# DeltaNet attention with a feed-forward block: other matmuls inside the bursts of 32x32 products, and state products with 48 weight columns

## The chip, the cores and the metric

The kernel runs on one core of a Trainium2 chip. The metric is the device time of that core in microseconds, for the whole launch. The tensor engine (TensorE, PE in the profile) multiplies and writes into PSUM; VectorE (DVE) and ScalarE (ACT) compute on SBUF and PSUM; GpSimd (POOL) has little to do here, and SyncE (SP) issues nearly all DMAs. A weight load of the tensor engine is listed separately as PEld.

## The reference

The first half is a delta rule with a running state per batch and head; its output, regrouped to tokens by features, goes through a feed-forward block with a learned slope for negative values.

```python
# q, k, v: (4, 8, 768, 48), beta: (4, 8, 768)
k_n = k / (norm(k) + 1e-6)
state = zeros((B, H, D, D))
for t in range(S):
    y[:, :, t] = einsum('bhd,bhde->bhe', q[:, :, t], state)
    v_old = einsum('bhde,bhd->bhe', state, k_n[:, :, t])
    state += beta_t * einsum('bhd,bhe->bhde', k_n[:, :, t], v[:, :, t] - v_old)
x = y.transpose(0, 2, 1, 3).reshape(3072, 384)
h = x @ w_in                                  # w_in: (384, 2048)
g = maximum(h, 0) + alpha * minimum(h, 0)
out = g @ w_out                               # w_out: (2048, 384)
```

Everything is float32.

## The kernel before

**Chunks and steps.** The sequence of 768 is cut into 12 chunks of 64 positions. A step `n` is one chunk of two of the four batches, so there are 24 steps, and the step's 16 problems (two batches, eight heads) are packed by halves of 64 partitions: `half(t)` is a half, `dims(a)` the first 48 partitions of one. Within a chunk the recurrence is a triangular system. Its matrix comes from products of keys with keys (`grams`), its inverse is built from blocks of 32, and then each step does: `through_state` (keys and queries times the state), `solve` (inverse times right side, giving `u`), `outputs`, and `next_state`, which adds keys times `u` to the state. `to_ffn` transposes the step's output into `xt`, the left operand of the feed-forward block.

**The 32x32 inverses.** Four steps form a group, whose 32x32 diagonal blocks VectorE inverts together by elimination. For the first group `eliminate_small` does only blocks of 16, and `cross` joins two inverted blocks of 16 into one of 32 by products of 32x32 weights with 16 columns, one per block and partition quarter: a burst at line 540, a copy by ScalarE (`half_way`), then two bursts at lines 549 and 555, and additions by VectorE (lines 561 and 563). `first_chunk` runs one `cross` over the blocks of the first two steps; two later ones, each over eight blocks, do steps 2 and 3. `between_1` and `between_2` (lines 621 and 636) then build the inverse of 64 from those of 32, with operands that ScalarE places by line 586.

**Fillers.** `busy(n)` (line 974) issues matmuls of the identity with 512 columns per unit of `n` into a PSUM tile that nobody reads. `first_chunk` calls it between its stages.

**Feed-forward.** `ffn_in(c)` multiplies `xt` of chunk `c` by `w_in` (line 809, 128x128 weights and 256 columns, 48 parts per chunk), twelve matmul records to a PSUM bank; ScalarE (line 819) and VectorE (line 821) then apply the activation and free the bank. Two banks alternate. `ffn_out` and `ffn_out_fast` (lines 851 and 873) multiply by `w_out`.

**Weights.** `w_in` and `w_out` come in pieces, fetched by SP (line 191) as space becomes free, and rewritten by ScalarE (lines 207, 208) and VectorE (lines 217, 222).

**Order.** Each engine runs its instructions in the order in which the program issues them: the schedule is written out by hand. `first_chunk` is straight code. After it, `weave` merges several generators: each has a number of parts, and the one whose share of parts done is smallest goes next, so that all of them advance evenly. The weave at line 1182 merges `ffn_in(0)`, the two later `cross` (taken alternately by `in_turn`, two parts each) followed by `ready(2)` and `pair(2)` (steps 2 and 3), the weight conversions, and the keys of the next group (`statics`). From step 4 on a loop weaves one step of attention with feed-forward parts and a share of the next group's elimination. All attention products use PSUM tiles `p_big`, of which there are three in rotation.

**A product in the trace.** Each float32 product appears as two weight loads and two matmul records, so 16 products of a step are 32 records. Only the transposes count once.

**The state.** `state[bp]` holds, for two batches, 48 rows in the first part of each half of 64 partitions; the keys of `k_late` are padded with zeros from 48 to 64 columns, so the product at line 707 fills 64 partitions of each half, and the rows beyond 48 are zero.

## Time and profile before

| | us |
|---|---|
| Median of 6 runs | 692.17 |
| Lowest and highest | 690.47 and 694.42 |
| The profiled execution's own time | 693.02 |
| Its span in the profile | 691.2 |
| Busy: TensorE, weight loads | 671.0, 581.9 |
| Busy: VectorE, ScalarE, GpSimd | 450.3, 248.7, 19.3 |
| Mean granted clock of TensorE | 0.985 |

The profile is one execution. Its page gives busy time by engine, a row of digits for 40 equal slices of the span (17.28 us each, with the granted clock in tenths in the row PEclk), the chain of work that ended last, and groups of instructions with their count, mean duration and the idle time before them. The ends of matmuls are modelled and neighbouring ones overlap, so the time from one start to the next is the better measure of what a product costs. "Issue" in a chain is time in which the engine waited for nothing that the profile shows. The times in rows of a stretch are microseconds from the start of the span.

### The profile page before, as it was taken

Reading aid. Unit: us, or ns where it says so; the run is one execution under the profiler, and the core shown is the slowest. Engines: PE = TensorE matmul, PEld = TensorE weight load, DVE = VectorE, ACT = ScalarE, POOL = GpSimd, SP = SyncE. Lnnn points to the kernel's source line nnn. Section 1 sums busy time; section 2 is a strip of 40 time slices with the busy share of each in tenths; the row PEclk is TensorE's granted clock in tenths of the full one; section 3 lists DMA queues with packets and bytes.
Section 4 is the critical chain, followed back from the end, with each engine's and each line's share of the span. In section 5 each row is a group of like instructions: output and inputs, shape, how many; then the busy total and the mean of one; then the engine's idle time right before and its main releaser. Section 6 shows DMA issues by size and latency. Waiting matters only on the chain.

```text
span 691.2 us, 22896 instructions
## 1 busy us (share of the span) xinstructions
PE 671.0 (97%) x10057; PEld 581.9 (84%) x10057; DVE 450.3 (65%) x1111; ACT 248.7 (36%) x592; POOL 19.3 (3%) x74
## 2 busy tenths in 40 slices
PE   6997999999999999999999999999999999999997
PEld 5576887756678989989988988988989989989997
DVE  5746679878988458867458867468867245245151
ACT  5826657424444234234234234124034033131120
POOL 4000001000000000000000000000000000000000
PEclk9959999999999999999999999999999999999999
DMA  8837654301322122122122101101201201100000
GB/s 138 227 102 185 147 139 126 76 24 28 68 49 47 21 52 48 22 51 47 22 51 37 37 25 36 37 25 36 40 24 34 47 22 29 36 1 2 24 1 23
DMA packets 110963, 37.76 MB, mean 55 GB/s; under 512 B 104160, under 2 KB 107248, under 8 KB 110864
## 3 DMA queue, kind: packets, MB, share of 16 engines
q1 hardware_dynamic: 109088, 35.81, 23.5%
q8 instruction: 79, 1.29, 0.8%
q10 hardware_dynamic: 1776, 0.49, 0.4%
q14 instruction: 20, 0.16, 0.1%
HBM read 31.56 MB, written 4.72 MB: 52 GB/s over the span
## 4 chain that ended last, share of the span: by engine, by line
PE 85%; DVE 8%; ACT 3%; issue 1%; DMA 1%; SPq 0%; ACTq 0%; DVEq 0%
PE p_ffn L809 35%; PE p_ffn L873 27%; PE p_big L664 3%; PE p_big L386 3%; PE p_big L353 2%; PE p_big L678 2%; PE p_big L691 2%; PE p_big L621 2%; PE p_big L636 2%; PE p_big L979 2%; DVE prod L470 1%; DVE block L476 1%; PE p_big L707 1%; PE p_ffn L851 1%; DMA ke<-in_k_dram 1%
## 5 line engine op out<-in xcount | busy, mean ns | idle before, releaser
L809 PE MATMUL p_ffn<-xt,w_in 128*128 128x256 f32 x1152 | 267.9, 386 | 3.1 <-DVE sums L821 1.4
L809 PEld LDWEIGHTS p_ffn<-xt,w_in 128*128 128x128 f32 x1152 | 213.4, 191 | 33.4 <-issue 2.3
L821 DVE SCALAR_TENSOR_TENSOR act<-act,al_t,p_ffn 128x256 f32<-128x256 f32 x176 | 76.5, 476 | 70.7 <-ACT act L819 69.6
L819 ACT ACTIVATE act<-p_ffn 128x512 f32<-128x512 f32 x88 | 52.3, 594 | 121.0 <-PE p_ffn L809 120.8
L873 PE MATMUL p_ffn<-w_out,act 128*128 128x192 f32 x480 | 83.7, 328 | 0.0
L873 PEld LDWEIGHTS p_ffn<-w_out,act 128*128 128x128 f32 x480 | 78.6, 190 | 0.9
L476 DVE TENSOR_TENSOR block<-block,prod 128x30 f32<-128x30 f32 (+9 forms) x150 | 49.8, 332 | 5.1
L470 DVE TENSOR_TENSOR prod<-block 128x30 f32<-128x30 f32 (+9 forms) x150 | 48.8, 325 | 2.0
L893 DVE TENSOR_TENSOR o_sb<-u,p_ffn 128x192 f32<-128x192 f32 x40 | 13.3, 352 | 42.1 <-PE p_ffn L873 35.9
L672 ACT COPY y<-p_big 128x384 f32<-128x384 f32 x22 | 10.5, 478 | 69.6 <-DVE r L667 69.6
L375 ACT COPY k_t<-p_big 128x512 f32<-128x512 f32 x24 | 13.9, 579 | 59.0 <-PE p_big L353 59.0
L375 ACT COPY q_t<-p_big 128x512 f32<-128x512 f32 x24 | 13.9, 589 | 56.9 <-PE p_big L353 56.9
L873 PE MATMUL p_ffn<-space_out,sums 128*128 128x192 f32 x160 | 29.3, 327 | 0.0
L873 PE MATMUL p_ffn<-more,sums 128*128 128x192 f32 x160 | 29.3, 327 | 0.0
L873 PE MATMUL p_ffn<-w_out,sums 128*128 128x192 f32 x160 | 27.7, 327 | 0.0
L873 PEld LDWEIGHTS p_ffn<-space_out,sums 128*128 128x128 f32 x160 | 26.6, 191 | 0.0
L873 PEld LDWEIGHTS p_ffn<-more,sums 128*128 128x128 f32 x160 | 26.6, 190 | 0.0
L586 ACT ACTIVATE diag<-inverse,which 64x128 f32<-64x128 f32 (+2 forms) x62 | 25.5, 412 | 2.2 <-DVE inverse L446 1.3
L893 DVE TENSOR_TENSOR u<-u,p_ffn 128x192 f32<-128x192 f32 x20 | 7.1, 353 | 29.3 <-PE p_ffn L873 29.3
L873 PEld LDWEIGHTS p_ffn<-w_out,sums 128*128 128x128 f32 x160 | 25.8, 191 | 0.0
L434 ACT COPY same<-right 32x256 f32<-32x256 f32 x32 | 12.9, 402 | 34.6 <-DVE right L395 34.4
L851 PE MATMUL p_ffn<-w_out,act 128*128 128x384 f32 x64 | 20.8, 487 | 0.0
(155 smaller groups left out, 952.6 us busy)
## 6 DMA issues: line engine op xcount, KB each, us to landing
w_out<-in_moe_w_in_dram SPq DMA_DIRECT2D x12, 512.0 KB, 5.5
qp<-in_q_dram SPq DMA_DIRECT2D x48, 96.0 KB, 3.0
v_raw<-in_v_dram SPq DMA_DIRECT2D x48, 96.0 KB, 2.9
kl<-in_k_dram SPq DMA_DIRECT2D x96, 48.0 KB, 2.5
out_dram<-o_sb SPq DMA_DIRECT2D x92, 48.0 KB, 1.7
space_out<-in_moe_w_out_dram SPq DMA_DIRECT2D x11, 384.0 KB, 4.3
ke<-in_k_dram SPq DMA_DIRECT2D x43, 96.0 KB, 3.1
w_out<-in_moe_w_out_dram SPq DMA_DIRECT2D x5, 384.0 KB, 4.3
```

Of the source, the lines that this page charges most:

```text
L375: nc.scalar.copy(dst.rearrange("p g i -> p (g i)"), src)
L386: nc.tensor.matmul(p[half(t ^ a if w else t), a, w, g], k_t[n][dims(a), g, half(t)], rhs[n][dims(a), g, half(t)],)
L470: nc.vector.tensor_tensor(out=prod, in0=r[:, 0:j, j : j + 1].to_broadcast([128, j, n]), in1=r[:, j : j + 1, j + 1 : HB].to_broadcast([128, ...
L476: nc.vector.tensor_tensor(out=r[:, 0:j, j + 1 : HB], in0=r[:, 0:j, j + 1 : HB], in1=prod, op=ALU.add)
L586: nc.scalar.mul(dst[n % NE][to or rows, a.start * G : a.stop * G, cols], src[m][rows, heads], which[rows, i : i + 1],)
L664: nc.tensor.matmul(p[half(t), a, w, g], x[n][dims(a), g, half(t)], state[bp][dims(a), t, g])
L809: nc.tensor.matmul(p_h[:, i], w_in[:, t, (f + i) * 128 : (f + i + 1) * 128], xt[:, t], start=(t == 0), stop=(t == KT - 1),)
L819: nc.scalar.activation(g, p_h, ACT.Relu, scale=-1.0)
L821: nc.vector.scalar_tensor_tensor(out=g[:, i], in0=g[:, i], scalar=al_t[:, f + i : f + i + 1], in1=p_h[:, i], op0=ALU.mult, op1=ALU.add,)
L851: nc.tensor.matmul(p_o[u], gs[f // 2][:, f % 2, u * 128 : (u + 1) * 128], w_out[:, f], start=(f == 0), stop=(f == FT - 1),)
L873: nc.tensor.matmul(p, x(i), w(i), start=(i == 0), stop=(i == FP - 1))
L893: nc.vector.tensor_tensor(out=to, in0=x, in1=p, op=ALU.add)
```

## The change

Three things are edited.

1. `cross` takes a further argument `aside`, a function that it calls between its products: after every fourth block of the bursts at lines 540 and 555, and after every eighth block of the burst at line 549.
2. In `first_chunk` that function issues a filler of half a unit (256 columns) at its first two calls after the first burst, and nothing at the calls after these. They write into the PSUM tile of the filler that stands between the two parts of the cross. The filler after the cross grows from 0.75 to 1.25 units. In the two later `cross`, the function advances `ffn_in(0)` by one part, five times per cross, so ten of its 48 parts are issued there; the weave gets the same generator with 38 parts as its count.
3. `next_state` uses 48 columns of the keys as weights instead of 64, so that its product fills the 48 rows in use, and updates the state by two subtractions on 48 partitions each, one per half, instead of one on 128 partitions.

With this the tensor engine's order in the later bursts alternates between 16 products of 32x32 (32 records) and one to four products of line 809; in the first cross it is 16 products of line 549, a filler, the other 16, a filler, and the 64 of line 555. No DMA is added or taken away.

```diff
-    def cross(m, bs, edge, half_way):
+    def cross(m, bs, edge, half_way, aside=None):
+        def let(b, every):
+            if aside is not None and b % every == every - 1:
+                aside()
 
         n = bs.stop - bs.start
         p = ps_one()[:, 0 : n * LB].rearrange("p (b i) -> p b i", i=LB)
...
                     turned[m][quad(i), bs.start + b, 0:LB],
                 )
+            let(b, 4)
         nc.scalar.copy(half_way[:, bs, 0:LB], p)
         yield
...
                     half_way[quad(i), bs.start + b, 0:LB],
                 )
+            let(b, 8)
...
                     inverse[m][quad(i), bs.start + b, LB:HB],
                 )
+            let(b, 4)
...
     def next_state(n):
...
-                    p[half(a), t, g], k_late[n % NKL][half(t ^ a), 2 * g + a],
+                    p[dims(a), t, g], k_late[n % NKL][half(t ^ a), 2 * g + a, 0:D],
                     us[n][half(t ^ a), a, g],
                 )
-            nc.vector.tensor_tensor(out=state[bp], in0=state[bp], in1=p, op=ALU.subtract)
+            for a in range(2):
+                x = state[bp][dims(a)]
+                nc.vector.tensor_tensor(out=x, in0=x, in1=p[dims(a)], op=ALU.subtract)
...
-        middle = cross(0, slice(0, 2 * H), edge, half_way)
+        waits, pause = iter([0.5] * 2), []
+        middle = cross(
+            0, slice(0, 2 * H), edge, half_way, lambda: pause and busy(next(waits, 0), pause[0])
+        )
         next(middle)
-        busy(1)
+        pause.append(ps_one())
+        busy(1, pause[0])
         begin_in(6)
         scale_v(0)
         next(middle)
-        busy(0.75)
+        busy(1.25)
...
-    later = [cross(0, slice(x * H, x * H + H), edge, half_way) for x in (2, 3)]
+    first_in = ffn_in(0)
+    later = [
+        cross(0, slice(x * H, x * H + H), edge, half_way, lambda: next(first_in, None))
+        for x in (2, 3)
+    ]
     weave(
-        (ffn_in(0), IN_PARTS), (chain(in_turn(*later), ready(2), pair(2)), 2 * CROSS + READY + PAIR),
+        (first_in, IN_PARTS - 10), (chain(in_turn(*later), ready(2), pair(2)), 2 * CROSS + READY + PAIR),
```

## The prediction

> **What bounds the kernel now.** I read the busy shares first, then the row of slices, the chain that ended last, and short stretches around the places where that chain leaves useful work.

> ```profile
> PE 671.0 (97%) x10057; PEld 581.9 (84%) x10057; DVE 450.3 (65%) x1111; ACT 248.7 (36%) x592; POOL 19.3 (3%) x74
> PEclk9959999999999999999999999999999999999999
> ```

> TensorE is busy 97% of the span, and only one slice (34.6 to 51.8 us) has a low granted clock. From 220 us on the tensor engine never pauses, so there only fewer or shorter matmul records can save time. The gain must be sought before 110 us. The chain there (start, duration, what; pieces left out):

> ```profile
> 30.47 1.05 PE p_big L979 x2
> 31.53 1.08 PE p_big L549 x61
> ...
> 32.98 0.72 issue
> 33.71 1.41 PE p_big L555 x68
> 35.12 1.58 PE p_big L979 x2
> 36.70 3.56 PE p_big L621 x64
> 40.25 2.00 PE p_ffn L979 x2
> 42.26 3.45 PE p_big L636 x62
> ...
> 47.56 2.00 PE p_ffn L979 x2
> ...
> 63.06 3.09 issue
> 66.15 0.23 PE p_big L555 x3
> 66.38 0.63 PE p_ffn L809 x2
> ...
> 72.59 1.93 PE p_big L621 x62
> ```

> Two things show. Inside both bursts of 32x32 products (L555) the engine stops for "issue", 0.72 and 3.09 us, though no semaphore holds it. And the same 64 records of L621 cost 3.56 us at 36.7 but 1.93 us at 72.6; a filler (L979, 512 columns, two records) costs 2.00 instead of 0.86. The stretches say why (columns: busy PE, PEld, DVE, ACT, POOL, clock, DMA share, GB/s):

> ```profile
> 32.00:34.00 2.00, 1.28 (x101) 1.17 (x98) 0.07 (x1) 1.38 (x3) 0.00 (x0) 0.84 0.57 103
> 34.00:36.00 2.00, 2.00 (x85) 1.51 (x77) 0.83 (x2) 0.00 (x0) 0.00 (x0) 0.50 0.55 109
> 50.00:52.00 2.00, 2.00 (x121) 1.95 (x115) 0.84 (x2) 0.90 (x2) 0.00 (x0) 0.90 0.67 244
> 66.00:68.00 2.00, 1.85 (x12) 1.59 (x13) 1.53 (x6) 0.51 (x1) 0.03 (x1) 0.87 0.99 308
> 68.00:70.00 2.00, 2.00 (x9) 1.72 (x8) 1.62 (x4) 1.17 (x4) 0.71 (x2) 0.50 0.91 321
> ```

> The clock is 0.50 from 33.4 to 50.4 us and from 67.4 to 70.9 us (the edges in finer cuts): 17.0 and 3.4 us, so whole windows of 3.41 us, each fall following a burst.

> **Why the clock falls.** [...] I weigh active cycles by the share of the array that a product uses. [...] The window 60.65 to 64.07, with 5.1 records of L809 at 512 cycles and 1.1 us of 32x32, gives 2800 and kept the clock. At the low clock, 2050 + 400 (filler, L636) did not raise it, and a window of filler, L678 and L691, some 3200, did. One threshold between 2450 and 2800 fits all. [...]

> **Part 1, the first cross (30 to 54 us).** Added: two 256-column fillers in the second burst, and the filler after it grows from 384 to 640 columns. An island of two full-array records among small products costs 0.63 us (the L809 pair at 66.38), against 2 x 0.216 in a run (18 records in 3.89 us): the 0.2 is the change of array shape. Worst windows now: from the end of the first filler to the big one, 64+1024+64+1024+240 = 2416; anything shifted by 0.15 us is above 2700. So most positions of the window keep the clock. The later gap, big filler to the next with L621 between, is about 2.6 us and leaves some 2900. With the clock kept, from 31.53 to the first L809 at 53.87 (22.34 us now): bursts without the stall 2.87, two islands 1.26, wait for VectorE's L561 and ScalarE's L586 1.5 (it covers the 640 columns, 1.1), L621 2.0, filler 1.0, L636 2.1 (1.05 per 32), L678 1.22, filler 1.0, L691 and L707 2.16, short filler 0.63, transposes and xt 1.27: 17.0. That is -5.3; VectorE (masks, v, conversions: 4.2 us after L563) ends just when L636 needs it. If that cover is short, L642 and L678 are late next.

> **The issue stops.** The instruction queue moved 79 packets of 16.3 KB. They start at 31.1 and 63.3 us, around the stops. Counting two instructions per record, stops one and two lie at the end of the 4th and 10th 256 instructions. A packet starts 0.7 to 4.2 us after the block before it was entered and is usable 2.7 us later. A block of 32x32 products lasts only about 2.8 us, so it outruns its successor. [...] In part 1 the second block comes 0 to 0.7 us late once the clock is high: +0.3. Part 1: -5.0 (range +2.5, clock lost, to -5.9).

> **Part 2, the later crosses (54 to 72 us).** Ten parts of ffn_in(0) move into the bursts; none is added. Bursts between full-array work rise from 4 to 10: six more changes at 0.2, +1.2. The block that lasted 2.9 us before the stop now lasts 4.6 against an arrival of 3.5 to 5.95: stop 0 to 1.35, I take 0.7 instead of 3.09. An island every 0.96 us gives 3600 per window, so the 3.46 us at half clock, worth 1.73, go. Sum: 1.2 + 0.7 - 3.09 - 1.73 = -2.9 (range +1.2 to -3.6). The weave has 38 instead of 48 parts over the rest of ready and pair, about 0.35 us less cover in each of 11 places; today nothing waits from 72 to 97 us, but the last L720 has only 0.7: +0.3 (0 to 1.5). No DMA is added; VectorE gets two act operations earlier, so two conversions later by 0.87, whose pieces are used over 10 us afterwards. SP's loads wait for those conversions and for the L707 products, and move with them.

> **Part 3, 48 weight columns.**

> ```profile
> L707 PE MATMUL p_big<-u,kl x704: 217/218/233, 50.4 to 589.7; 64*64 64x48 f32 x176
> L711 DVE TENSOR_TENSOR state<-state,p_big x22: 546/554/556, 51.2 to 590.1; 128x384 f32<-128x384 f32 x22
> ```

> A group of 32 records takes 467 ns from first to next: four records per 58 ns, near a load of 64 columns. No product with 48 columns is in the trace. Loads take 104 ns with 32 columns, 135 with 64, 190 with 128, so some 14 less with 48. Bounds per group: 0 (issue sets the pace) and -117 (a quarter); four 32x32 records take 35 to 49 ns, so I take -80. If a 48-column shape counted as a change of shape, +200; 48-row products (L386 between L678 and L636, 0.48 us) show none, and I keep it for the range. In the 17 groups where TensorE alone sets the pace: -1.4 (+3.4 to -2.0).

> **Part 4, the update in two.** Each has 384 elements per partition as before, so costs the same 0.47 us of queue: 22 x 0.47 = 10.3 us more VectorE. Behind it wait L403, L329, then L821, which frees a bank of ffn_in. In the elimination stretches (313 us) L821 starts the moment the queue is free, and the bank is taken 0.89 us after it ends: 0.46 fits. Without that cover it would cost 0.46 at each of 15 steps. Two places have only 0.15: L821 at 105 and 210 us. +0.6 (0.3 to 2.5).

> **Sum.** -5.0 - 2.9 + 0.3 - 1.4 + 0.6 = -8.4. The profiled execution took 693.02 us (span 691.2): 684.6. It is 0.85 above the median, 692.17; the runs spread over 4 us, as the windows' position would make them, so I take 684.5 as the median.

> **Rivals.** *Clock still lost in the first cross*: the window can fall on the weak 3.4 us, or a late block widens the gap to the filler above 2.75 us. Then part 1 is 0 to +2.5, -1 with a partial loss: about 689. For it: 2416 against a threshold of 2450 or more; against: only a narrow position hits it. *Nothing measurable*: instructions arrive at DMA's pace, islands sit in what was stall, and the clock falls: -2.0 + 1.5 + 0.3 - 1.4 + 0.6 = about 691. *Slower*: the monitor does not credit pieces of 0.43 us, and the low clock extends over both bursts. Then part 1 costs +2.4, and the 40 records of L809 between 54 and 67 us cost 0.216 more each, +8.6, less the 4.8 of stop and old low clock, +1.2, -0.8 for the rest: 692.2 + 6.6 = 699. It decides once threshold exceeds 3600 cycles; the window kept at 2800 speaks against it.

> **How the numbers follow.** A measurement here can tell about 0.3%, 2.1 us. Kept clock 0.57 (681.5 to 687.5), lost in the first cross 0.22 (687 to 690.5), nothing measurable 0.10 (690 to 694), slower 0.11 with DVE or shape costs above their ranges included. So faster 0.79, same 0.10, slower 0.11. Range 681.5 to 690.5: it leaves out both last cases.

> **What would show it.** Right: clock 1.00 from 32 to 50 us, L621 about 2.0 us for 64 records, the first L809 near 48.5 us, an issue stop under 1.4 us in the later bursts, no low clock near 67 us, 32 records of the state product in about 0.39 us, no new waits on L821's successor after 220 us. Wrong: a clock of 0.50 after the first burst, a stop still near 3 us, a first L809 record slowed after 48-column products, or TensorE pauses behind the second update.

## The result, and the profile after

The changed kernel takes 687.16 us (median of 37 runs, 685.68 to 694.5), the kernel before 691.17 us (74 runs). The ratio of paired runs is 0.9951, with a 95% interval of 0.9938 to 0.9964: 3.4 us less by the ratio, 4.0 between the medians. That is clear of no change and inside the stated range, but only about half of the 7.7 us forecast. The profiled execution took 687.16 us, with a span of 685.3. Two single runs further down, of 865 and 762 us at a mean clock of 0.754 and 0.855, are left out of the medians.

First the page of the changed kernel: busy shares, and the clock of the 40 slices.

```profile
PE 665.3 (97%) x10063; PEld 574.1 (84%) x10063; DVE 462.1 (67%) x1133; ACT 248.6 (36%) x592; POOL 19.3 (3%) x74
PEclk9999999999999999999999999999999999999999
```

The slice with half clock is gone; VectorE is busy 12 us longer, for 22 more operations. The chain that ended last, from the first cross to the later ones (start, duration, what):

```profile
33.03 0.61 PE p_big L555 x32
33.64 0.63 PE p_big L989 x2
34.27 0.61 PE p_big L555 x32
34.88 0.63 PE p_big L989 x2
35.51 1.22 PE p_big L562 x85
...
38.19 2.06 PE p_big L629 x64
40.25 1.05 PE p_ffn L989 x2
41.30 1.93 PE p_big L644 x62
...
46.98 0.45 issue
...
50.07 0.70 PE p_ffn L819 x2
50.77 0.37 PE p_big L545 x32
51.14 0.63 PE p_ffn L819 x2
...
68.18 1.92 PE p_big L629 x61
```

An island of two records costs 0.63 us as forecast, the 64 records of L629 (L621 before) take 2.06 instead of 3.56 us, and both long stops are gone; a new one of 0.45 us stands at 47 us. The stretches (columns as before, the clock third from the end):

```profile
34.00:36.00 2.00, 2.00 (x102) 1.45 (x104) 0.00 (x0) 0.87 (x2) 0.00 (x0) 1.00 0.63 117
68.00:70.00 2.00, 2.00 (x70) 1.90 (x71) 1.21 (x3) 1.89 (x4) 0.50 (x2) 1.00 0.59 118
```

And the state product with its update:

```profile
L715 PE MATMUL p_big<-u,kl x704: 204/205/241, 46.1 to 583.9; 64*48 64x48 f32 x176
L721 DVE TENSOR_TENSOR state<-state,p_big x44: 536/551/558, 46.8 to 584.8; 48x384 f32<-48x384 f32 x44
```

With 48 partitions instead of 128 an operation costs VectorE the same time, 551 against 554 ns, so two of them cost twice as much. What that second operation delays is seen in TensorE's waits between 90 and 220 us (engine, line, what it waited for; total, times, longest). Before:

```profile
PE p_ffn L809 <- DVE sums L821: 1.4, 1, 1.4
PE p_big L353 <- DVE y L698: 1.4, 1, 1.4
PE p_big L636 <- ACT mid L626: 0.8, 1, 0.8
PE p_ffn L809 <- DVE act L821: 0.6, 1, 0.6
PE p_ffn L809 <- DVE prod L470: 0.5, 1, 0.5
```

After:

```profile
PE p_ffn L819 <- DVE act L831: 2.1, 3, 1.0
PE p_big L353 <- DVE y L706: 1.5, 1, 1.5
PE p_ffn L819 <- DVE sums L831: 1.4, 1, 1.4
PE p_ffn L819 <- DVE prod L470: 1.0, 1, 1.0
PE p_big L644 <- ACT mid L634: 0.8, 1, 0.8
PE p_big L730 <- DVE state L721: 0.3, 1, 0.3
```

The waits for VectorE grow from 3.9 to 6.3 us, by some 2.4 us. Cut at the same matmul records, the two profiled executions compare so:

| From, to | before | after |
|---|---|---|
| start to the first burst | 28.85 | 30.36 |
| first burst to the first feed-forward product | 25.03 | 19.71 |
| to the first L621 (L629) after it | 18.65 | 18.03, with 12 more feed-forward records |
| to L636 (L644) near 155 us (150 us after) | 83.16 | 81.89 |
| to a record near 220 us, the same in both | 63.84 | 64.99 |
| to the last matmul | 467.63 | 466.31 |

The start, where nothing was edited, has no part in the change: the clock first rises at 23.1 us in one execution and 25.7 in the other, and the fillers there take 8.40 and 9.44 us. In the runs below, the first burst begins between 28.8 and 29.8 us with or without the change.

### The profile page after: what moved, and what is told of

The parts are those of the page before. It is cut to its first block, busy times and chain, and to the rows that moved or that the text cites. A ratio compares the mean times of both kernels' runs of the same rounds, so it can differ in the third digit from the quotient of the medians.

```text
span 685.3 us, 22945 instructions
## 1 busy us (share of the span) xinstructions
PE 665.3 (97%) x10063; PEld 574.1 (84%) x10063; DVE 462.1 (67%) x1133; ACT 248.6 (36%) x592; POOL 19.3 (3%) x74
## 4 chain that ended last, share of the span: by engine, by line
PE 84%; DVE 10%; ACT 3%; issue 1%; DMA 1%; ACTq 0%; SPq 0%; DVEq 0%
PE p_ffn L819 35%; PE p_ffn L883 27%; PE p_big L672 3%; PE p_big L386 3%; PE p_big L353 2%; PE p_big L699 2%; PE p_big L686 2%; PE p_big L644 2%; PE p_big L629 2%; PE p_big L989 2%; DVE block L476 2%; DVE prod L470 2%; PE p_big L715 1%; PE p_ffn L861 1%; PE p_big L730 1%
## 5 line engine op out<-in xcount | busy, mean ns | idle before, releaser
L819 PE MATMUL p_ffn<-xt,w_in 128*128 128x256 f32 x1152 | 269.1, 385 | 5.1 <-DVE act L831 2.1
L819 PEld LDWEIGHTS p_ffn<-xt,w_in 128*128 128x128 f32 x1152 | 212.2, 190 | 35.8 <-issue 3.6
L883 PEld LDWEIGHTS p_ffn<-space_out,sums 128*128 128x128 f32 x160 | 26.6, 190 | 0.0
L883 PEld LDWEIGHTS p_ffn<-more,sums 128*128 128x128 f32 x160 | 26.6, 190 | 0.0
L434 ACT COPY same<-right 32x256 f32<-32x256 f32 x32 | 12.9, 402 | 34.6 <-DVE right L395 34.4
L721 DVE TENSOR_TENSOR state<-state,p_big 48x384 f32<-48x384 f32 x44 | 24.1, 548 | 1.3 <-PE p_big L715 0.9
```

The costliest lines, as they stand in the source:

```text
L721: nc.vector.tensor_tensor(out=x, in0=x, in1=p[dims(a)], op=ALU.subtract)
L819: nc.tensor.matmul(p_h[:, i], w_in[:, t, (f + i) * 128 : (f + i + 1) * 128], xt[:, t], start=(t == 0), stop=(t == KT - 1),)
L883: nc.tensor.matmul(p, x(i), w(i), start=(i == 0), stop=(i == FP - 1))
```

## The experiments

Ratios are to the kernel before, run beside each experiment, with 95% intervals; times are medians.

**The bursts alone** (state product and update as before).

```diff
-                    p[dims(a), t, g], k_late[n % NKL][half(t ^ a), 2 * g + a, 0:D],
+                    p[half(a), t, g], k_late[n % NKL][half(t ^ a), 2 * g + a],
...
-            for a in range(2):
-                x = state[bp][dims(a)]
-                nc.vector.tensor_tensor(out=x, in0=x, in1=p[dims(a)], op=ALU.subtract)
+            nc.vector.tensor_tensor(out=state[bp], in0=state[bp], in1=p, op=ALU.subtract)
```

> The changed kernel with the state product and its update as before (64 weight columns, one subtraction): fillers and feed-forward parts in the bursts alone. My theory (the gain is made in the bursts, by the clock and by the supply of instructions; the state part saves about 0.11 us at each of 17 steps and gives back 1.1 to 1.5 us to VectorE): within 0.5 us of the changed kernel, about 687.6; the clock stays at 1.00 and no pause of 3 us. Rival (the shorter weight loads make up half of the gain or more): 689 or above.

Measured: 686.28 us, ratio 0.9931 (0.9914 to 0.9948). The whole gain is made in the bursts. The state part is no gain: without it the kernel is about 0.9 us faster by the medians, 1.4 by the ratios, but the intervals overlap.

**The state part alone**, put into the kernel before.

```diff
+                    p[dims(a), t, g], k_late[n % NKL][half(t ^ a), 2 * g + a, 0:D],
...
+            for a in range(2):
+                x = state[bp][dims(a)]
+                nc.vector.tensor_tensor(out=x, in0=x, in1=p[dims(a)], op=ALU.subtract)
```

> The kernel before with the state product and update of the changed one alone. My theory: 32 records take 0.36 instead of 0.47 us, minus 1.9 us in all, and VectorE's second update costs 1.5 us between 90 and 220 us: 690.8, hardly distinguishable from before. The rival of the shorter loads: 689.5 or below. A third, that the second update delays the feed-forward's banks throughout: above 692.

Measured: 691.87 us, ratio 1.0003 (0.998 to 1.0026): nothing, as expected, and of two opposite terms. In its trace the stretch after 220 us is 1.60 us shorter than before, those between 70 and 220 us are 2.16 us longer (84.17 and 64.99 us against 83.16 and 63.84).

**The second update without the shorter loads.**

```diff
-                    p[dims(a), t, g], k_late[n % NKL][half(t ^ a), 2 * g + a, 0:D],
+                    p[half(a), t, g], k_late[n % NKL][half(t ^ a), 2 * g + a],
```

> The changed kernel with 64 weight columns again but the update still in two operations of 48 partitions: the second update without its gain. My theory: the first run of this study (one update, 64 columns) plus 1.5 us, about 689.1, with new tensor pauses behind VectorE only near 95 and 190 to 220 us. Rival (the second operation is hidden everywhere): equal to the run with one update, 687.6. Rival (it delays every step): plus 5 us or more.

Measured: 689.14 us, ratio 0.9979 (0.9951 to 1.0007), so 2.9 us over the run with one update where 1.5 was expected. TensorE's waits between 90 and 220 us, first with one update, then with two:

```profile
PE p_ffn L817 <- DVE act L829: 0.9, 2, 0.6
...
PE p_ffn L817 <- DVE prod L470: 0.5, 1, 0.5
```

```profile
PE p_ffn L819 <- DVE act L831: 2.0, 3, 0.9
...
PE p_ffn L819 <- DVE prod L470: 1.0, 1, 1.0
```

Counted from record to record, 2.2 us of the difference lie in three places: 0.85 between 93 and 100 us (steps 2 and 3), 0.69 near 198 us and 0.68 near 206 us. The rest arises before 50 us. After 220 us both take 467.63 us: there the second operation costs nothing.

**48 columns only where TensorE alone sets the pace.**

```diff
-                    p[dims(a), t, g], k_late[n % NKL][half(t ^ a), 2 * g + a, 0:D],
+                    p[dims(a) if n >= 7 else half(a), t, g],
+                    k_late[n % NKL][half(t ^ a), 2 * g + a, 0 : D if n >= 7 else C],
...
-            for a in range(2):
-                x = state[bp][dims(a)]
-                nc.vector.tensor_tensor(out=x, in0=x, in1=p[dims(a)], op=ALU.subtract)
+            for rows in (dims(0), dims(1)) if n >= 7 else (slice(0, 128),):
+                x = state[bp][rows]
+                nc.vector.tensor_tensor(out=x, in0=x, in1=p[rows], op=ALU.subtract)
```

> The changed kernel, but up to step 6 the state keeps 64 weight columns and one update; 48 columns and two updates from step 7 on, where TensorE alone sets the pace. My theory: the loss of 1.1 to 1.5 us behind VectorE goes and nearly all of the shorter loads' gain stays: 685.9, with the step from 186 to 214 us of the changed kernel back to some 27.2 us between the through-state products. Rival (the later tensor pauses near 200 us have another cause, such as later loads or conversions): no different from the changed kernel, 687.2.

Measured: 684.23 us, ratio 0.9905 (0.9886 to 0.9925): better than either kernel. Its waits between 90 and 220 us fall back to

```profile
PE p_ffn L820 <- DVE act L832: 0.9, 2, 0.6
...
PE p_ffn L820 <- DVE prod L470: 0.5, 1, 0.5
```

and the stretch after 220 us keeps the 466.04 us of the shorter loads. So VectorE's loss is in the steps up to 6 and the gain in those from 7 on, and the two can be had apart.

**No islands in the first cross.**

```diff
-        waits, pause = iter([0.5] * 2), []
+        waits, pause = iter([0.0] * 2), []
...
-        busy(1.25)
+        busy(0.75)
```

> The changed kernel without the two fillers in the first cross and with the filler behind it at 384 columns again. My theory (clock by weighted activity): the clock falls to 0.50 near 33 us and stays there for some 17 us; from the end of the long filler to the first feed-forward product 25 us instead of 19.6; median about 691.5. [...]

Measured: 691.14 us, ratio 0.9995 (0.9975 to 1.0015). Part 1 is worth 3 to 4 us between the medians. The clock falls as before (columns as above):

```profile
36.00:38.00 2.00, 1.83 (x34) 1.83 (x36) 2.00 (x7) 0.51 (x2) 0.00 (x0) 0.55 0.00 0
40.00:42.00 2.00, 2.00 (x8) 0.49 (x8) 0.00 (x0) 1.41 (x4) 0.00 (x0) 0.50 0.71 256
48.00:50.00 2.00, 2.00 (x46) 0.97 (x48) 0.32 (x1) 0.00 (x0) 0.00 (x0) 0.54 0.26 51
```

The low clock lasted from 36.2 to 49.9 us, four times 3.41 us, not five (17.07 us before), and the stretch from the first burst to the first feed-forward product took 24.35 us. No idle gap between the first burst and the fall was longer than 0.9 us, so no long pause of TensorE explains the fall. The run takes the longer filler behind the cross away together with the islands and does not part the two; in the execution before, the clock fell at 33.3 us, ahead of that filler (35.1 us).

**No islands in the later crosses.**

```diff
-        cross(0, slice(x * H, x * H + H), edge, half_way, lambda: next(first_in, None))
+        cross(0, slice(x * H, x * H + H), edge, half_way, None)
...
-        (first_in, IN_PARTS - 10), ...
+        (first_in, IN_PARTS), ...
```

> The changed kernel with the later crosses as before (their bursts whole, the feed-forward's 48 parts woven as before). My theory (instruction supply): an issue pause of 2 to 3.5 us comes back near the end of the later bursts, in most runs followed by a window at half clock; plus 3.2 us, about 690.4. Rival (instructions are always fetched in time and the pause was an accident of one profile): no pause; faster by the six changes of shape, 686.

Measured: 688.74 us, ratio 0.9966 (0.9942 to 0.9989). The stop comes back, at half its length in the profile of before, and with it one cold window of 3.4 us (61.6 to 65.1 us):

```profile
58.20 0.63 PE L562 MATMUL p_big<-inverse,act 32*32 32x16 f32 x52
60.43 0.29 PE L562 MATMUL p_big<-inverse,act 32*32 32x16 f32 x10 [1.60 <-issue]
```

```profile
62.00:64.00 2.00, 2.00 (x8) 1.59 (x7) 1.47 (x5) 1.41 (x3) 0.74 (x2) 0.50 0.95 314
```

Part 2 is worth 1.0 us by the ratios and 1.6 between the medians, where I expected 3.2; the intervals of this run and of the changed kernel overlap. The same stop measured 3.1 us before, 1.5 with the state part alone and 3.2 in the shifted run below: over four profiled executions, each of another kernel, it varies by 1.7 us.

**Islands of half the size.**

```diff
-        waits, pause = iter([0.5] * 2), []
+        waits, pause = iter([0.25] * 2), []
```

> The changed kernel with the two fillers in the first cross at 128 columns each instead of 256. My theory (a threshold of 2450 to 2800 weighted cycles per 3.41 us): the weakest window then holds about 1400 to 1900, below the threshold wherever the window lies, so the clock falls as without islands: 691 and a clock of 0.50 for some 17 us. Rival (the islands matter by giving the instruction supply time, or any full-array product resets the monitor): the clock stays, about 687.

Measured: 687.23 us, ratio 0.9961 (0.9935 to 0.9986), and a clock of 1.00 through the burst of the profiled execution:

```profile
30.00:34.00 4.00, 4.00 (x145) 2.83 (x146) 2.43 (x6) 3.25 (x6) 0.00 (x0) 1.00 0.49 82
34.00:38.00 4.00, 3.60 (x168) 2.88 (x168) 2.41 (x7) 0.91 (x2) 0.00 (x0) 1.00 0.67 119
```

7 of the 12 runs kept it (0.995 or above); the other five, at 0.987 to 0.993, took 690.2 to 693.4 us. I expected the clock to fall always. My threshold is refuted; that full-array work among the products holds the clock is not. The islands take away the first stop (0.72 us before) as well, so no run has the one without the other; but idle time does not sort the windows: one with 0.36 us of it lost the clock (29.9 to 33.3 us before), one with 1.00 us kept it (60.65 to 64.07 us before).

My weights do not sort them either: one filler and 118 records of 32x32, some 2280 by those weights, lost the clock before (29.9 to 33.3 us); one filler and 160 records, some 2370, kept it in the run without first islands. Both lie under the threshold of 2450 or more. Threshold and weights were my estimate, and by what rule the clock is granted no run shows.

**Another place in the instruction stream.** 32 more small products at the start of the kernel before, in time in which TensorE waits for loads.

```diff
+    for _ in range(32):
+        nc.tensor.matmul(ffn_banks[0][0:HB, 0:LB], ident[0:HB, 0:HB], ident[0:HB, 0:LB])
     squares(0)
     betas()
```

> The kernel before with 32 more products of 32x32 (64 records, 128 instructions) at its very start, in time in which TensorE waits for the first loads; their result is not read. My theory (blocks of 256 instructions, fetched one ahead): the issue pauses move by 64 records towards the start of the stream: the first from the 38th record of line 555 to about the 38th of the products just before it (line 549), the second from the end of the last later burst into its first third. Rival (the pause belongs to the products of line 555 themselves): it stays at the same record of that line. Time near that of before, 691.

Measured: 695.72 us in a single run. The timeline of TensorE around the stops (start, duration, group, idle time before it):

```profile
31.82 0.80 PE L549 MATMUL p_big<-act,inverse 32*32 32x16 f32 x39
33.37 0.52 PE L549 MATMUL p_big<-act,inverse 32*32 32x16 f32 x22 [0.75 <-issue]
...
33.77 1.34 PE L555 MATMUL p_big<-inverse,act 32*32 32x16 f32 x100
37.64 0.55 PE L555 MATMUL p_big<-inverse,act 32*32 32x16 f32 x25 [2.53 <-issue]
...
64.00 0.64 PE L549 MATMUL p_big<-act,inverse 32*32 32x16 f32 x29
67.83 0.20 PE L549 MATMUL p_big<-act,inverse 32*32 32x16 f32 x2 [3.19 <-issue]
```

Before, the stops came after the 471st and the 1236th matmul record of the stream; here, with 64 records more ahead of them, after the 472nd and the 1236th again, which are now other products. They belong to the place in the stream, not to the products. A third stop, 2.53 us, opens after the 600th, 128 records or 256 loads and products behind the first, and ends 2.2 us after a packet of the instruction queue starts (35.40 us). Had it been an accident of line 555, none would have moved. Where the stops fall can cost time: in this execution, with its third stop, the stretch from the first burst to the first feed-forward product is 1.6 us longer than before. That the kernel as a whole is slower is not shown, since one run of 695.72 us lies within the range of the kernel before (up to 696.61).

**A longer filler**, on the kernel with 48 columns from step 7 on.

```diff
-        busy(1.25)
+        busy(1.65)
```

> The kernel with 48 columns from step 7 on, with the filler behind the first cross at 845 columns in all instead of 640; it grows into time in which TensorE waits for VectorE and ScalarE. Theory (the clock is still lost in some runs because the 2.4 us of small products between this filler and the next leave a window of about 3000 weighted cycles, on the threshold): the same median, 684.5, or 0.1 us more, and no run of about twelve with a mean clock under 0.995, where the changed kernel had some 6 of 38. Rival (the runs with a lost clock have another weak place): one or more of twelve at 0.993 or below and at 688 or above.

Measured: 684.65 us, ratio 0.9901 (0.987 to 0.9933): the same within the intervals. None of 6 runs lost the clock (means of 0.999 and 1.000), but the kernel without it has none among its five runs of 684.0 to 685.1 us either (0.994 to 1.000), so this does not tell where the changed kernel still loses it.

## Why the prediction was right, and where it was too large

**The clock in the first cross: right.** Over all profiles, the stretch from the first burst to the first feed-forward product takes 24.35 to 25.24 us without islands (26.6 in the shifted run, with its third stop) and 19.71 to 20.94 with them (21.56 with the longest filler), 4.6 on average against 5.0 forecast. The late second block that I put at 0 to 0.7 us appeared, further on: 0.45 us at 47 us, 0.95 in the run of the bursts alone. The argument was right in kind: products of the full array in the burst held the clock at 1.00. The threshold and its weights were an estimate, and the run with half islands refuted them. The rival of a clock still lost was given 0.22, and 6 of the 37 runs of the changed kernel lie above 690 us, five of them with a mean clock of 0.980 to 0.993. Nor is the clock always lost without islands: one run of the kernel before and one of the state part alone took 688.15 and 688.51 us at a mean clock of 0.998 and 0.997, too high for the long fall (13.7 us at half clock take 0.010 off the mean over 689 us), and 6 of the 74 runs before took only 685.1 to 687.4 us (at clocks that are not known). So the islands make the fall rarer, and part of the forecast gain was there in some runs before.

**The later crosses: right in kind, too large.** No stop and no cold window were left after the change; the twelve feed-forward records that moved ahead are worth 2.6 us, so the stretch to L621 gained 3.2 us where 2.9 was forecast. But the term of the stop to be saved was too large: I took 3.09 us from one execution, and others show 1.5, 1.6 and 3.2. Part 2 as a whole gives 1.0 to 1.6. The 2.8 us that I gave a block of 32x32 products include a filler: 128 such records take 1.40 us in the run with half islands, about half of the 2.6 and 2.8 us that passed in the execution before from the start of a packet to the end of a stop.

**The weight columns: right.** 32 records take 360 ns instead of 467, -107, near my outer bound of -117; forecast was -80. The stretch after 220 us is 1.60 us shorter in the run of that part alone. The feared change of shape for 48 columns did not appear.

**VectorE's second update: the step that failed.** It is hidden after 220 us, as worked out from the slack of 0.89 us. Before that the prediction counts 0.3 us at each of two places with little slack, +0.6 in all (range to 2.5); it was 0.85 + 0.69 + 0.68 = 2.2 us, at three places. At the first, two updates (steps 2 and 3) come one shortly behind the other. VectorE's idle time ahead of the activation between them, 0.85 us before, was 0.37 us in the run of the bursts alone and none with two updates, so it could not absorb the first. The place near 198 us has no term in the prediction. VectorE stands idle for 0.56 us ahead of it before, waiting for ScalarE's L819, but that idle time was no cover for the update ten microseconds earlier. TensorE's wait for that bank grew, before and after:

```profile
203.72 2.40 PE L809 MATMUL p_ffn<-xt,w_in 128*128 128x256 f32 x10 [0.52 <-DVE prod L470]
```

```profile
198.56 2.40 PE L819 MATMUL p_ffn<-xt,w_in 128*128 128x256 f32 x10 [0.98 <-DVE prod L470]
```

The delay was passed on, not absorbed. The run from step 7 on shows the size by itself: removing both terms up to step 6 gives back 2.9 us by the medians.

**The base.** My sum started from a profiled execution of 693.02 us, and its long stop was probably part of what made it slow (not shown): the median is 691.17. I moved the sum by only 0.1 us for that. Between the two profiled executions the terms add up: -5.3 (first cross) - 1.9 (from there to 150 us, with VectorE's first 0.9 in it) + 1.2 (to 220 us) - 1.3 (rest) + 1.5 (the start) = -5.8, against 685.3 - 691.2 = -5.9. Between medians 3.4 to 4.0 remain. The rest of the difference, about 2 us, I put down to the chance of single executions: the length of the stop, the clock's windows, the start. No run here shows how much each takes at the median.

## What to carry to other kernels

Here small products cost more than their own time: a clock of 0.50 for 13.7 to 17.1 us came after whole bursts of them, and stops of 0.7 to 3.2 us within. Full-array work that has to be done anyway was better placed among them than behind them (1.0 to 1.6 us in the later crosses). An operation added to a busy engine, VectorE in this case, should be priced stretch by stretch: here it was free in the last two thirds of the kernel and cost 2.2 us in the rest, more than the 1.6 us that the shorter weights save, and doing it only where it is free (684.23 us) beats both versions. And where single executions differ by more than the effect, a saving read off one profile should be shrunk to what several profiles share.

## What the runs showed of the hardware

Products with 48 weight columns were faster than those with 64: loads of 122 against 135 ns, and 32 records in 360 against 467 ns, with no pause at the change between the two: near 200 us L699 to L715 takes 0.50 us from start to start and L386 to the next L819 (L817) 0.59, in the changed kernel as in the run of the bursts alone.

Two fillers of 128 columns, 0.42 us each from start to start, among 2.5 us of 32x32 products held the clock in 7 of 12 runs; without any it was lost in each of the 12 runs of that kernel, by their mean clocks of 0.983 to 0.990.
